# Another sequence of units in the first batch, with a newly written order of every engine

## The chip, the cores and the metric

The kernel runs on one core of a Trainium2 chip. Its engines are TensorE (PE in the profile; PEld are its weight loads), VectorE (DVE), ScalarE (ACT), GpSimd (POOL), and SyncE (SP), which here only issues transfers. The metric is the device time of one execution in microseconds (us). The kernel before ran three times: 225.64, 225.78 and 225.80 us, median 225.78 us.

## The reference, cut to what matters

```python
# q, k, v: (4 batches, 8 heads, 768 tokens, 64); centroids: (8, 16, 64)
q_assign = argmax(normalised(q) @ normalised(centroids))      # the same for k_assign
mask   = q_assign[:, :, :, None] == k_assign[:, :, None, :]
scores = where(mask, q @ k.T / 8, -1e9)
attn   = softmax(scores);  x = attn @ v                       # tokens x 512
h    = x @ w_in                                               # 512 -> 1024
solu = h * softmax(h)
ln   = (solu - mean) / sqrt(var + 1e-6) * g_ln
out  = ln @ w_out                                             # 1024 -> 512
```

All arrays are float32; the result is 3072 x 512.

## The kernel before, in words

Heads are worked in pairs: a batch has pairs 0 to 3. For each pair of heads, queries and keys are loaded, turned so that the head's 64 numbers lie on partitions, and written in bf16 into a tile `qk`. Sixteen (with a second group, 32) further rows of `qk` hold the one-hot cluster of each token, so that one matmul of 80 or 96 rows gives the score with its mask. The exponential of the score then goes through ScalarE, and a second matmul multiplies it with the values. The tokens' normalised result goes through the feed-forward part, one tile of 128 tokens at a time (24 tiles).

The code records every step as a named operation, and this document uses the names. A dotted name gives batch and pair, then the side (0 queries, 1 keys) and the head of the pair or the half.

| name | step | function, line | engine |
|---|---|---|---|
| `ld`, `lv` | load queries/keys, values | `load`, `load_apart` L374, `load_v` L527 | SP |
| `tp`, `xa` | batch 0: turn 128 x 384 on PE into the region `hreg`; copy it to `xt` | L386; `keep_tokens` L393 | PE; ACT or DVE |
| `xt` | later batches: turn on DVE | `turn` L407 | DVE |
| `ca` | cast `xt` into `qk` | `cast` L431, L433, L435 | POOL, DVE, ACT |
| `cl` | cluster scores | `clusters` L445, L450 | PE |
| `tb`, `mx`, `oh`, `ot` | turn back, maximum, one-hot, turn | L459, L472, L478/L484, L491/L494 | DVE |
| `pl`, `bl` | copy the one-hot rows into `qk`; blank 16 rows for the pair's second head | L506/L514; L523 | POOL, DVE, SP (a transfer); POOL, DVE |
| `cv` | cast values | L532 | POOL, DVE |
| `S n.k`, `E n.k` | bank k of unit n: scores, exponential | `scores` L601, `expo` L607 | PE; ACT |
| `V n.j`, `N g` | values of unit n; division for group g | L624; L636, L649 | PE; DVE |
| `su`, `sk`, `me`, `ce`, `wi` | preparation of the feed-forward weights | L574, L581, L584, L587, L552 | PE, DVE, POOL |
| `h`, `hm`, `ex`, `u` | x @ w_in, maximum, exponential, product | L710, L716, L722, L727 | PE, DVE, ACT, DVE |
| `bn`, `ag`, `at`, `al` | variance and factor | L738, L742, L748, L754/L757 | DVE, DVE, POOL, POOL |
| `tx`, `tu` | turn x, u by a transfer | `turn_x`, `f_turn` L732 | SP |
| `y`, `sc`, `ou` | u @ w_out, scaling, store | L771, L786/L788, L798 | PE, ACT or DVE, SP |

Units. A unit is one piece of scores: pair 0 of batch 0 has units 0 to 3 with six or three banks of 384 columns; all later units have three banks of 512 columns. In batch 0 the units of pairs 1 to 3 come as the list `FIRST` (L280) says: its entry (p, s) stands for two units, one for each head of pair p, with the s-th third of the queries. `BANKS` is the sequence of all score banks. `S` and `E` follow it strictly, and the `V` follow the units.

Rings. Scores have three PSUM banks (`ring_s`, L1012), so `S` of a bank waits for the `E` three banks earlier. The exponentials have nine tiles (`ring_e`), so `E` of a bank waits for the `V` that read the tile nine banks earlier. All values of a group share one PSUM tile `ops`, so the first `V` of a group waits for the `N` of the group before. The region `hreg` has three banks; in batch 0 each `tp` waits for the `xa` three before it.

Order. Nothing is scheduled at run time: each engine runs its instructions strictly in the order written in `ORDER`, one text for each engine, in which "S3 tp2" means the next three `S` and the next two `tp` (`queues`, L110). An operation whose input is late therefore holds up everything behind it on its engine. `AWAY` (L73 on) moves single operations from the engine that the code gives them by default to another that can run them. Feed-forward work (`h`, `y`) comes to PE only when the first batch is nearly through, from 46 us on.

Of the kernel before, what the change touches and what calls it, by code (L numbers as in the profile page):

```python
# [22 lines left out]
class Weave:  # L23
# [6 lines left out]
        ld4 lv si ld4 lv lg ld4 lv2 ld4 lo2 ld4 lo ld3 lo ld3 li4 tx ld3 lv3 tx ld4 tu ld9 lv ld tu  # L30
        tx ld3 tu ld3 ou ld2 ou ld tu ld12 tu ld4 lv ld2 ou tx ld3 tu ou ld2 tx lv ld tu ld4 tx ld
        tu ou2 ld lv ld4 tu ld4 tu ld ou ld7 pl ou ld lv2 ld3 tu lv tx ou tu lv pl ld4 ou2 tx lv tu
        tx ou tu pl2 tu2 tx tu tx ou2 tx ou tu tx2 ou tu2 ou2 tu2 ou6
# [8 lines left out]
    """
    ORDER["PE"] = """
        wm tp2 cp tp cl tp fl5 cl fl4 S3 tp2 S2 tp S cq S tp S2 tp2 S2 V3 S cl S tp2 V3 S gt S tp S
        tp S2 cl S2 V2 S V S2 tp S2 tp S2 V2 S V S2 cl S2 V2 S V2 S3 V S2 V2 S2 V S cl S3 su S2 V3 S
# [1 line left out]
        S h S V S V S h S2 V3 S2 V h S2 h V2 S y3 S2 h3 S3 y V3 h V S2 V2 S cl S3 h2 S2 V3 S y2 S V
        h2 S V y2 S h S V h S2 h S y3 S2 y V3 h S3 cl V2 S V S y S2 y2 S3 V3 S y S2 V3 S2 cl S V S2
        V2 S h S2 V2 S V S h S2 V2 cl V2 S3 y2 S V S2 V y S2 y V2 S3 h2 S V h S h S2 V h S V S V y2
        S h V y2 S2 V S h3 S cl V S2 V2 S h V cl S3 h2 V y V S3 y2 V S h V3 S y S h S2 h2 S3 V2 y h  # L50
        S V S2 y V3 y S3 h3 y S3 V3 S h S V S V cl S V S h S cl V2 S3 y V2 S y S2 y V2 S3 h y V S3 V
# [1198 lines left out]
```

## Time and profile before

| | us |
|---|---|
| median of three runs | 225.78 |
| the profiled execution | 225.95 |
| its span, first to last instruction | 223.9 |
| around the span (225.95 - 223.9) | 2.05 |
| PE busy in the span | 215.1 |
| DVE / ACT / POOL busy | 197.3 / 191.5 / 127.1 |

A busy PE isn't one at its peak: a score of 256 columns takes 264 ns in the mean there, but consecutive ones overlap. How far PE is from idle is better read from the distance of one matmul's start to the next. Rows of the timeline give start, duration, engine, line, operation, the tiles written and read with their shapes, a count, and in brackets the idle time of the engine before it with what ended it. One row can stand for several instructions that follow each other; its time is then that of the first start to the last end.

### The profile page before, as it was taken

The page shows a single profiled execution, that of the slowest core. Times are in us where ns is not written, and L with a number is a line of the kernel's source. Part 1 is how long each engine was busy: PE and PEld are TensorE (multiplying, and loading weights), DVE is VectorE, ACT ScalarE, POOL GpSimd, SP SyncE. Part 2 cuts the span into 40 slices and gives each one's busy share as a digit, 9 for nine tenths or more (in the row PEclk, how much of TensorE's full clock was granted, in tenths as well). Part 3 has the DMA queues.
Part 4 walks back from the last instruction along what each step waited for, and adds up shares of the span by engine and source line. Part 5 has one row for each costly group of instructions (what it writes and reads, how often), then busy time and mean ns, then how long its engine had stood idle before and what let it go on. Part 6 is the DMA issues. An engine that isn't in the chain of part 4 may idle for free.

```text
span 223.9 us, 6574 instructions
## 1 busy us (share of the span) xinstructions
PE 215.1 (96%) x2388; PEld 148.1 (66%) x2420; DVE 197.3 (88%) x359; ACT 191.5 (86%) x371; POOL 127.1 (57%) x247
## 2 busy tenths in 40 slices
PE   7899999999999999999999999999999999999993
PEld 3576756677667678776677667777677687754442
DVE  3799899899999989999998989887998889888981
ACT  3689999999998999998889899999999998982362
POOL 3489843964794999547668634943895413031331
PEclk9999999999999999999999999999999999999999
DMA  7998989999898989999999999199931433766622
GB/s 152 353 318 147 249 199 275 290 243 158 132 199 140 232 130 165 193 189 177 183 218 168 184 195 195 65 174 232 236 64 28 79 70 120 96 146 170 176 97 94
DMA packets 125679, 38.80 MB, mean 173 GB/s; under 512 B 115016, under 2 KB 121168, under 8 KB 125648
## 3 DMA queue, kind: packets, MB, share of 16 engines
q1 hardware_dynamic: 123904, 37.87, 80.6%
q10 hardware_dynamic: 1744, 0.52, 1.0%
q8 instruction: 19, 0.31, 0.6%
q14 instruction: 12, 0.10, 0.2%
HBM read 23.11 MB, written 6.29 MB: 131 GB/s over the span
## 4 chain that ended last, share of the span: by engine, by line
PE 86%; ACT 5%; DVE 3%; issue 3%; DMA 1%; POOL 1%; ACTq 0%; DVEq 0%; POOLq 0%
PE sps L601 28%; PE hreg L710 18%; PE yps L771 16%; PE ops L624 14%; ACT e L607 5%; PE csc L450 4%; PE hreg L386 2%; PE hreg L574 1%; PE hreg L771 1%; DMA c_all<-in_centroids_dram 1%; PE csc L445 1%; DVE bs L738 1%; DVE u L727 1%; ACT xt L393 0%; PE hreg L584 0%
## 5 line engine op out<-in xcount | busy, mean ns | idle before, releaser
L607 ACT ACTIVATE e<-sps 128x512 bf16<-128x512 f32 (+1 forms) x294 | 151.0, 599 | 12.2 <-PE sps L601 10.2
L601 PE MATMUL sps<-qk 80*128 80x256 bf16 (+5 forms) x636 | 93.8, 264 | 1.8 <-POOL qk L514 0.7
L601 PEld LDWEIGHTS <-qk 80*128 80x128 bf16 (+1 forms) x636 | 60.2, 121 | 27.9 <-issue 9.0
L624 PEld LDWEIGHTS <-e 128*128 128x128 bf16 x1152 | 50.4, 97 | 12.3 <-issue 1.9
L624 PE MATMUL ops<-v,e 128*128 128x65 bf16 x1152 | 55.0, 193 | 0.1
L710 PE MATMUL hreg<-w_in_sb,xT 128*128 128x512 bf16 x173 | 49.1, 379 | 1.1
L771 PE MATMUL yps<-w_out_c,uT 128*128 128x512 bf16 x171 | 46.4, 379 | 0.6
L727 DVE TENSOR_TENSOR u<-e_sb,hreg 128x1024 bf16<-128x1024 bf16 x24 | 29.0, 1210 | 4.9 <-ACT e_sb L722 4.7
L514 POOL COPY qk<-oht 32x384 f32<-32x384 f32 (+1 forms) x50 | 24.4, 488 | 15.8 <-DVE oht L494 13.6
L738 DVE BATCH_NORM_STATS2 bs<-u 128x6 f32<-128x512 bf16 x48 | 31.5, 676 | 0.2
L716 DVE TENSOR_REDUCE nmax<-hreg 128x1 f32<-128x1024 f32 x24 | 29.0, 1209 | 2.6 <-PE hreg L710 2.2
L722 ACT ACTIVATE e_sb<-hreg,nmax 128x1024 bf16<-128x1024 f32 x24 | 26.9, 1120 | 4.5 <-DVE nmax L716 4.4
L433 POOL CAST qk<-xt 64x768 bf16<-64x768 f32 (+1 forms) x31 | 26.1, 842 | 5.5 <-DVE xt L393 3.9
L771 PEld LDWEIGHTS <-uT 128*128 128x128 bf16 x200 | 18.2, 97 | 12.3 <-DVE uT L704 0.7
L754 POOL TENSOR_SCALAR esq<-es,mv 128x1 f32<-128x1 f32 x24 | 8.5, 355 | 29.0 <-DVE mv L742 20.8
L435 POOL TENSOR_SCALAR qk<-xt 64x768 bf16<-64x768 f32 (+1 forms) x28 | 23.0, 820 | 1.7
L710 PEld LDWEIGHTS <-xT 128*128 128x128 bf16 x192 | 16.8, 97 | 9.4 <-issue 0.6
L407 DVE STREAM_TRANSPOSE xt<-raw 128x768 f32<-128x768 f32 x24 | 22.6, 953 | 0.2 <-DMA raw<-in_q_dram 0.2
L748 POOL TENSOR_SCALAR es<-esum 128x1 f32<-128x1 f32 x24 | 5.3, 221 | 27.6 <-ACT e_sb L722 27.1
L649 DVE TENSOR_TENSOR x<-ops,den 128x256 bf16<-128x256 f32 (+1 forms) x39 | 18.9, 486 | 1.3
L757 POOL TENSOR_TENSOR alpha<-esq,halves 128x1 f32<-128x1 f32 x24 | 13.5, 561 | 2.0
L786 ACT ACTIVATE y<-yps,alpha 128x512 f32<-128x512 f32 x13 | 9.0, 692 | 6.4 <-PE yps L771 6.0
(80 smaller groups left out, 170.1 us busy)
## 6 DMA issues: line engine op xcount, KB each, us to landing
vf<-in_v_dram SPq DMA_DIRECT2D x16, 384.0 KB, 4.4
out_dram<-y SPq DMA_DIRECT2D x23, 256.0 KB, 2.7
raw<-in_q_dram SPq DMA_DIRECT2D x50, 96.0 KB, 3.7
raw<-in_k_dram SPq DMA_DIRECT2D x50, 96.0 KB, 3.0
w_g<-in_moe_w_out_dram SPq DMA_DIRECT2D x4, 512.0 KB, 5.3
w_st<-in_moe_w_in_dram SPq DMA_DIRECT2D x4, 512.0 KB, 5.9
raw<-in_q_dram SPq DMA_DIRECT2D x3, 384.0 KB, 6.3
raw<-in_k_dram SPq DMA_DIRECT2D x3, 384.0 KB, 6.8
```

Source lines behind the costliest of these rows:

```text
L433: VEC[e].tensor_copy(dst, src)
L435: VEC[e].tensor_scalar(dst, src, scalar1=inv_C, scalar2=1.0, op0=Alu.mult, op1=Alu.mult)
L514: ins = VEC[e].tensor_copy(dst.bitcast(F32), src.bitcast(F32).unsqueeze(1) .to_broadcast([NB, 2, n // 2]))
L601: nc.tensor.matmul(sps_[n, k][:, c0:c0 + w], side(b, h // 2, 1, h % 2, keys)[r], side(b, h // 2, 0, h % 2, slice(s0 * P, s0 * P + w))[r])
L607: nc.scalar.activation(es[n, k][:, :w], sps_[n, k][:, :w], Act.Exp, scale=exp_scale, bias=-exp_scale)
L624: nc.tensor.matmul(opss[g][:, s, :VW], es[n, k][:, c0:c0 + P], v1[slot(b, h // 2)][:, h % 2, kt, :VW], start=(kt == 0), stop=(kt == n_t - 1))
L710: uses(nc.tensor.matmul(hreg[:, at(f, f2)[1], :], xTs[f][:, dc, :], w_in_sb[:, dc, f2 * FF2:(f2 + 1) * FF2], start=(dc == 0), stop=(dc == ...
L716: uses(nc.vector.tensor_reduce(ff[f, "nmax"][:], pair_of(f), axis=AXY, op=Alu.max, negate=True), *both(f))
L722: uses(nc.scalar.activation(ff[f, "e"][:], pair_of(f), Act.Exp, bias=ff[f, "nmax"][:], accum_out=ff[f, "esum"][:]), *both(f))
L727: uses(nc.vector.tensor_tensor(ff[f, "u"][:], ff[f, "e"][:], pair_of(f), op=Alu.mult), *both(f))
L738: nc.vector.bn_stats(ff[f, "bs"][:, f2, :], ff[f, "u"][:, f2, :])
L771: ins = nc.tensor.matmul(dst, ff[f, "uT"][:, at(f, f2)[0] * (n_fc // 2) + c, :], w_out_c[:, fc, cols], start=(fc == 0), stop=(fc == n_fc - 1))
```

## The change

The list `FIRST` changes, and with it every text of `ORDER` and both the members and the engines of `AWAY`. No operation is added or removed; no size, tile or buffer changes.

```diff
-    FIRST = [(p, s) for p in range(1, n_pair) for s in range(2)] + [(p, 2) for p in range(1, n_pair)]
+
+    FIRST = [(1, 0), (1, 1), (2, 0), (3, 0), (2, 1), (3, 1), (1, 2), (2, 2), (3, 2)]
```

Written out, the list before is (1,0), (1,1), (2,0), (2,1), (3,0), (3,1), (1,2), (2,2), (3,2). The two lists differ in one exchange: the first third of pair 3 and the second third of pair 2 change places. Pair 3 is then needed from unit 10 on, where it was needed from unit 12 on; units 10 to 13 are renumbered, and units 4 to 9 and from 14 on are what they were.

The core of the order's diff, with the beginning of each text:

```diff
     ORDER["POOL"] = """
-        po z ca2 pl2 cv z bl pl2 ca z ca pl2 ca z2 ca3 cv ca cv ca pl3 sg ca cv2 pl3 ca2 gs pl ca cv
-        ca wi ca pl2 wi3 bl ca pl2 cv at cv pl ca pl al bl at cv ca pl ca pl cv ca3 al at ca al ca
...
+        po ca2 pl2 ca bl zo pl2 bl ca pl ca4 cv2 ca pl2 z ca2 gs ca pl3 z ca pl3 cv2 pl sg z2 ca3 pl
+        wi4 pl2 ca3 pl2 at pl2 cv bl2 cv at z cv ca al ca al at al pl2 cv pl2 ca4 at cv pl ca pl3 al
...
     ORDER["PE"] = """
-        wm tp2 cp tp cl tp fl5 cl fl4 S3 tp2 S2 tp S cq S tp S2 tp2 S2 V3 S cl S tp2 V3 S gt S tp S
...
+        wm tp2 cp tp cl tp fl5 cl fl4 S3 cq tp S2 tp S2 tp S tp S2 tp2 V3 S2 cl S2 V3 S gt tp S tp
...
     ORDER["DVE"] = """
-        cn cb xa ca tb mx oh ot pl2 tb mx oh ot xa3 bl cf cv xa zo xa2 tb ca mx oh gk N ot tb pl mx
...
+        cn xa cb ca tb mx oh ot pl2 tb mx oh ot cv pl xa cv xa3 ca cf tb mx N oh xa cv ot gk pl xa
...
     ORDER["ACT"] = """
-        wa xa2 ca2 xa ca2 E12 xa2 E6 xa E58 ex E12 ex E8 ex E8 ex E3 sc E5 ca E2 ex E25 ex E9 sc E6
...
+        wa xa2 ca xa ca3 E9 xa2 E9 xa2 E5 xa E3 xa E50 ex E10 ex E7 ex E2 sc E3 ca E ex ca E6 sc E8
...
```

With the names filled in, this is where the orders differ at the places that the next part speaks of (a semicolon parts before and after):

- PE up to the first values: `S1.2 cq S0.3 tp0.1.1.1 S0.4 S0.5 tp0.2.0.0 tp0.2.0.1 S1.3 S1.4 V0.0`; now `S1.2 S0.3 tp0.1.1.0 S0.4 tp0.1.1.1 S0.5 S1.3 tp0.2.0.0 tp0.2.0.1 V0.0`.
- PE before unit 25: `S24.0 S24.1 V22.0 V22.1 V23.0 S24.2 S25.0`; now `S24.0 S24.1 h2.0.0 h2.0.1 S24.2 S25.0`, with the three values behind `S25.1`.
- ACT at the start: `xa0.0.0.0 xa0.0.1.0 ca0.0.0.0.0 ca0.0.0.1.1 xa0.0.1.1 ...`; now `xa0.0.1.0 xa0.0.0.1 ca0.0.1.0.0 xa0.0.1.1 ...`. Before `E6.0` ACT had three more copies (`xa0.2.1.0`, `xa0.2.1.1` before `E2.0`, `xa0.3.0.0` before `E3.0`); now it has six: `xa0.2.0.0`, `xa0.2.0.1` between `E0.5` and `E1.3`, `xa0.2.1.1`, `xa0.3.0.0` before `E3.0`, `xa0.3.1.0` before `E3.5`, `xa0.3.1.1` before `E4.2`.
- DVE at the start: `cb xa0.0.0.1 ca0.0.1.0.0 tb0.0.0`; now `xa0.0.0.0 cb ca0.0.0.0.0 tb0.0.0`. Behind `ot0.0.1`: `xa0.1.0.0 xa0.1.0.1 xa0.1.1.0`; now `cv0.0.0 pl0.0.1.1.0 xa0.1.0.0 cv0.0.1 xa0.1.0.1 xa0.1.1.0`.
- DVE around pair 3: `N2 xt1.0.0 mx0.3 xt1.0.1 N3 oh0.3 ot0.3`; now `tb0.3 mx0.3 oh0.3 ot0.3 N2 pl0.3.1.0 ca0.3.1.1 xt1.0.0 xt1.0.1 N3`. The cast `ca0.3.1.1` was POOL's.
- DVE around the first product: `u0 oh1.1 ot1.1`; now `oh1.1 N9 u0 ot1.1`.
- POOL behind the weight casts: `wi3 bl1.0 ca1.0.1.1 pl1.0.0.0 pl1.0.0.1 cv1.0.0`; now, behind `wi3`, `pl1.0.1.1 pl1.0.0.0 ca1.1.0.0 ca1.1.0.1 ca1.1.1.0 pl1.0.0.1 pl1.1.1.0 at0 pl1.1.1.1 pl1.1.0.1 cv1.0.0 bl1.0`.
- SP: the values of pairs 1 and 2 in batch 0 are loaded ahead of the keys of pair 3; `pl1.1.0.0` stands behind `tu0`.
- The end of PE's order, from `ptx23`, has one `h` less in it, which now stands before; behind that the two are the same.

Between engines, 63 operations change place:

| from | to | operations |
|---|---|---|
| POOL | DVE | 18: 8 `cv`, 5 `ca`, 3 `pl`, 2 `bl` |
| DVE | POOL | 13: 4 `pl`, 4 `bl`, 2 `ca`, 2 `cv`, `zo` |
| DVE | ACT | 10: 5 `xa`, 2 `ca`, 3 `sc` |
| ACT | DVE | 6: 2 `xa`, 1 `ca`, 3 `sc` |
| POOL | SP | 8 `pl` (`pl1.1.0.0` and seven of batches 2 and 3) |
| SP | POOL | 2 `pl` |
| POOL | ACT | 4 `ca` (1.2.0.0, 1.2.0.1, 3.0.1.0 and one of pair 0) |
| ACT | POOL | 2 `ca` |

In all DVE has 10 `xa` before and 7 now, 5 `cv` before and 11 now, 4 `ca` before and 6 now; ACT has 6 `xa` before and 9 now, 5 `ca` before and 8 now; POOL has 212 operations before and 199 now; SP has 4 `pl` before and 10 now. PE has the same 732.

More of the change, by code (lines that the diff above doesn't have):

```diff
@@ L29 @@
     ORDER["SP"] = """
[L30 to L33, printed above, removed]
+        ld4 lv si ld4 lg ld lv2 ld lv ld3 lo ld3 lo ld lo ld5 lo ld4 li4 tx ld5 lv ld tx ld7 tu lv
+        ld2 pl tx ld tu ld3 ou ld2 tu ld lv2 ld2 tu ld ou lv ld13 tu ld2 lv ld3 ou tx ld3 tu ld2 ou
@@ L47 @@
[L47 to L51, printed above, removed]
```

70 lines of the change are left out of this document (39 added, 31 removed).

## Prediction

> **What bounds the kernel now.** I read the page's header, its busy times and the chain of waits first.
>
> ```profile
> span 223.9 us, 6574 instructions
> PE 215.1 (96%) x2388; PEld 148.1 (66%) x2420; DVE 197.3 (88%) x359; ACT 191.5 (86%) x371; POOL 127.1 (57%) x247
> PE 86%; ACT 5%; DVE 3%; issue 3%; DMA 1%; POOL 1%; ACTq 0%; DVEq 0%; POOLq 0%
> ```
>
> The chain that ends last runs through PE for 86% of the span. The change gives PE the same 732 operations, so time can only come from stretches in which PE waits. Where these are, the stage windows say (columns: busy us of PE, PEld, DVE, ACT and POOL, counts in brackets, PE's granted clock, DMA share, GB/s).
>
> ```profile
> 10.00:55.00 45.00, 43.70 (x544) 30.32 (x547) 41.22 (x85) 42.01 (x89) 30.59 (x54) 1.00 1.01 241
> 55.00:210.00 155.00, 153.40 (x1740) 108.49 (x1768) 142.50 (x242) 139.06 (x265) 90.01 (x170) 1.00 0.82 156
> ```
>
> From 55 to 210 us PE is busy for 153.40 of 155 us: a new order can hardly gain there, it can only lose. The first 55 us are different. ACT is busy for 42.01 of 45 us there, and until feed-forward work comes PE has little to do that doesn't follow from an exponential. ACT's timeline shows where it waits.
>
> ```profile
> 10.52 3.56 ACT L607 ACTIVATE e<-sps 128x384 bf16<-128x384 f32 x9 [1.11 <-PE sps L601]
> 14.80 1.25 ACT L607 ACTIVATE e<-sps 128x384 bf16<-128x384 f32 x3 [0.72 <-PE ops L624]
> 16.44 0.86 ACT L393 COPY xt<-hreg 128x384 f32<-128x384 f32 x2 [0.39 <-PE hreg L386]
> ...
> 25.91 5.50 ACT L607 ACTIVATE e<-sps 128x512 bf16<-128x512 f32 x11 [0.16 <-PE sps L601]
> 31.57 1.57 ACT L607 ACTIVATE e<-sps 128x512 bf16<-128x512 f32 x3 [0.16 <-PE sps L601]
> 33.33 4.69 ACT L607 ACTIVATE e<-sps 128x512 bf16<-128x512 f32 x9 [0.18 <-PE sps L601]
> 38.39 6.23 ACT L607 ACTIVATE e<-sps 128x512 bf16<-128x512 f32 x12 [0.38 <-PE sps L601]
> 44.79 5.55 ACT L607 ACTIVATE e<-sps 128x512 bf16<-128x512 f32 x11 [0.16 <-PE sps L601]
> ```
>
> Between the first exponential and 55 us ACT waits 0.72 + 0.39 + 0.16 + 0.16 + 0.18 + 0.38 + 0.16 = 2.15 us in all. So two things decide: when `E0.0` starts, and what ACT has to do beside exponentials until PE is full of feed-forward work.
>
> **The change, part by part.** Sums are made against the profiled execution, 225.95 us (span 223.9 and 2.05 around it); the median of the runs is 0.17 lower, and a difference found here is laid on the median, 225.78.
>
> *Start of the first score.* These rows are the way to it.
>
> ```profile
> 6.74 0.53 PE L450 MATMUL csc<-xt,c_bd 128*32 128x192 f32 x8
> 6.85 0.56 DVE L393 COPY xt<-hreg 128x384 f32<-128x384 f32 x1 [0.66 <-PE hreg L386]
> 7.32 0.34 DVE L435 TENSOR_SCALAR qk<-xt 64x384 bf16<-64x384 f32 x1
> 7.59 0.37 DVE L459 STREAM_TRANSPOSE cst<-csc 128x192 f32<-128x192 f32 x1
> 10.16 0.65 PE L601 MATMUL sps<-qk 80*128 80x384 bf16 x3 [0.73 <-POOL qk L514]
> ```
>
> The cluster scores end at 7.27, but their turning stands behind a copy and a cast on DVE and starts at 7.59. Both go to ACT; what DVE gets in their place (`xa0.0.0.0`, `ca0.0.0.0.0`) reads the first turning, which ACT copies today ahead of all this. The turning then starts at about 7.31, and all steps behind it on the way keep their lengths: -0.28 at `S0.0` and `E0.0`. Bounds: 0, if PE's clusters start later, and -0.28.
>
> *The first values.* Behind that, DVE gets work ahead of the copies that free `hreg`.
>
> ```profile
> 9.25 0.58 DVE L514 COPY qk<-oht 32x192 f32<-32x192 f32 x2
> 11.35 1.45 DVE L393 COPY xt<-hreg 128x384 f32<-128x384 f32 x3
> 13.49 0.51 DVE L532 CAST v<-vf 128x384 bf16<-128x384 f32 x1
> 13.14 0.82 PE L386 MATMUL hreg<-ident_f,raw 128*128 128x128 f32 x6
> 14.12 0.73 PE L624 MATMUL ops<-v,e 128*128 128x65 bf16 x18
> ```
>
> Two value casts of 0.51 and one placing of 0.58 / 2 = 0.29, 1.31 us, come in front of the third copy. It ends at 12.80 - 0.28 + 1.31 = 13.83. `tp0.2.0.1` needs the bank that it frees, and takes 0.82 less the 0.33 by which the other `tp` starts sooner, 0.49. `V0.0` stands right behind it: 13.83 + 0.49 = 14.32, against 14.12. The gain of 0.28 is gone there and 0.20 is lost. Every `E` behind the ninth tile waits for these values. Bounds: -0.28 (the copies in time after all) and +0.20.
>
> *Three more copies on ACT.* By shape, a copy takes
>
> ```profile
> L393 ACT COPY xt<-hreg 128x384 f32<-128x384 f32 x6 | 2.8, 477 | 1.3 <-PE hreg L386 1.3
> ```
>
> 3 x 0.477 = 1.43 us on the engine that paces this stretch. Two of the six now stand in the wait of 0.72 before `E1.3`, and the wait of 0.39 before the old copies has no copy to wait for any more: 1.43 - 1.11 = +0.32. With the +0.20, `E6.0` (25.91 before) comes 0.52 later. Behind it ACT waits 0.16 + 0.16 + 0.18 + 0.38 + 0.16 = 1.04 us more, each time since PE had a block of other work (`cl`, `su`, `me`) in front of a score. An ACT that runs half a microsecond later gives PE that much lead over it, and these waits shrink; I take 0.40 of them, between 0 (PE falls behind equally) and 1.04. Left at 55 us: +0.12.
>
> *Pair 3 one unit sooner.* `S10.0` is now pair 3 and needs `ca0.3.1.1`.
>
> ```profile
> 32.96 0.83 POOL L435 TENSOR_SCALAR qk<-xt 64x768 bf16<-64x768 f32 x1
> 31.08 0.83 PE L601 MATMUL sps<-qk 80*128 80x256 bf16 x6
> 31.26 0.98 DVE L491 STREAM_TRANSPOSE w_out_c<-w_out_c 128x768 bf16<-128x768 bf16 x1
> 27.91 0.98 DVE L407 STREAM_TRANSPOSE xt<-raw 128x768 f32<-128x768 f32 x1 [0.21 <-DMA raw<-in_q_dram]
> 27.05 0.18 DVE L636 RECIPROCAL den<-ops 128x4 f32<-128x4 f32 x1 [0.38 <-PE ops L624]
> 27.27 0.42 DVE L649 TENSOR_TENSOR x<-ops,den 128x256 bf16<-128x256 f32 x1
> ```
>
> That cast ended on POOL at 33.79, and `S10.0` is the second bank of the PE row, at 31.31. `ot0.3` ended at 32.24. Two turnings of 0.98 and two divisions of 0.60 now come behind it: 32.24 - 3.16 = 29.08. Then come one division (0.60), a placing and the cast, for which I set POOL's times, 0.50 (a row below) and 0.83: 31.01. It is ready 0.3 us before `S10.0`, so the exchange costs nothing, and gains nothing either: the same scores, banks and values pass in another sequence. Without that cover it costs what the second rival says.
>
> *A wait at unit 25.* `bl1.0` now stands behind the placings of pair 1, which wait for `ot1.1`.
>
> ```profile
> 51.60 1.22 DVE L727 TENSOR_TENSOR u<-e_sb,hreg 128x1024 bf16<-128x1024 bf16 x1 [0.34 <-ACT e_sb L722]
> 53.33 0.58 DVE L494 STREAM_TRANSPOSE oht<-oh 128x384 bf16<-128x384 bf16 x1
> 54.04 0.50 POOL L514 COPY qk<-oht 32x384 f32<-32x384 f32 x1 [1.70 <-DVE oht L494]
> 51.65 0.24 POOL L748 TENSOR_SCALAR es<-esum 128x1 f32<-128x1 f32 x1 [2.93 <-ACT e_sb L722]
> 57.11 0.41 POOL L523 MEMSET qk<- 16x384 f32 x1
> 55.84 0.62 PE L601 MATMUL sps<-qk 80*128 80x256 bf16 x4
> ```
>
> `ot1.1` right behind `u0` ends at 51.60 + 1.22 + 0.58 = 53.40, and POOL can start 0.13 behind it, as today (54.04 after 53.91): 53.53. Three placings of 0.50, the small operation (0.24), a value cast (0.51, as on DVE above) and the blanking (0.41) make 2.66: `bl1.0` ends at 56.19, or somewhat later with the steps between them. `S25.0` is the second bank of the PE row, at 55.84 + 0.22 = 56.06. The wait is 0.13 if its place on PE stays, and less as two parts of `h` take the place of three values in front of it; I take +0.10. Bounds: 0, and 0.64, if `ot1.1` keeps its old end at 53.91. Behind a blocked `S25.0` stand the bank `S25.1` and the values of units 22 and 23, which need nothing more from POOL but wait in PE's order.
>
> *The rest.* From 55 to 210 us I take 0. ACT gets four casts and three scalings more and gives one cast and three scalings away, out of 155 - 139.06 = 15.9 us that it is idle there. Bounds: -1.6, all that PE is idle there (155 - 153.40), and +0.6, one more wait like that at unit 25. Eight placings go to SP and two leave it; there one lands late:
>
> ```profile
> qk<-oht SPq DMA_DIRECT2D x4, 48.0 KB, 2.2
> ```
>
> 2.2 us against 0.50 on POOL, which is 1.7 later but off POOL's queue; all but `pl1.1.0.0` are in batches 2 and 3, where a pair is prepared units ahead. The end of PE's order is the same but for one `h`: 0.
>
> Sum: 0.20 + 0.32 - 0.40 + 0.10 = +0.22, 226.00 us. With one term at a time at its bound (the waits behind `E6.0` at 1.04 or 0, unit 25 at 0.64) it is 225.4 to 226.6; the low bound of the rest belongs to the faster rival.
>
> A POOL cast can be stretched by DVE: a 64 x 768 cast took 1.15 us at 34.31 while DVE cast the same shape from 34.03 to 34.77.
>
> ```profile
> 34.31 1.15 POOL L433 CAST qk<-xt 64x768 bf16<-64x768 f32 x1
> 34.03 0.74 DVE L433 CAST qk<-xt 64x768 bf16<-64x768 f32 x1
> ```
>
> [...]
>
> **The rivals.** *Faster: ACT's waits fill up.* If the copies go into waits entirely, all 2.15 us of them are gone for 1.43 us of copies, and the first score comes 0.28 sooner: 1.43 - 2.15 - 0.28 = -1.00, 224.78. For it: DVE is relieved of copies and its 41.22 of 45 us loosen. Against it: the waits behind 25 us come from PE's blocks, which the change only puts elsewhere.
>
> *Slower: the exchange takes away pair 3's cover.* If `ca0.3.1.1` is no sooner than today (33.8), `S10.0` waits 33.8 - 31.3 = 2.5 us; three banks at 0.49 (5.50 / 11) keep ACT going for 1.5 of it: +1.0, 226.8. It decides once the cast ends after 31.3, with 0.3 us to spare. That the pair is needed sooner but isn't ready sooner is also the case in which the change doesn't do what it says.
>
> *Slower: ACT is the bound and takes the copies in full.* 1.43 - 0.28 = +1.15, 226.93. It decides once the copies on ACT wait for their `tp`, so that they fill no wait. For it: ACT is the busiest engine but PE from 10 to 55 us. Against it: two copies stand exactly in the widest wait. [...]
>
> **How the numbers follow.** About 0.2% (0.45 us) can be told from no change here. Forecast 226.00: 0.40, of it 0.26 within that, 0.10 slower, 0.04 faster. ACT's waits filled: 0.30, faster. Pair 3 late: 0.10, slower. Copies in full: 0.20, slower. So faster 0.34, same 0.26, slower 0.40. The forecast's own range is 225.4 to 226.6; the range for 8 in 10 goes from 224.7, where the faster rival lies, to 227.3, the fullest copies with the wait at unit 25.
>
> **What would show it.** In the changed profile: `S0.0` near 9.88 and `V0.0` near 14.3; ACT's row before the fourth set of 384-column exponentials with copies where 0.72 us of waiting was; the first 512-column exponential near 26.4; a wait of PE for POOL's blanking near 56.2; 155 us of full PE behind it. A first 512-column exponential before 25.5 would make the forecast wrong to the fast side, a PE wait over 0.5 us for a cast near 31 or anywhere behind 60 us to the slow side.

## The result, and the profile after

| | before | after |
|---|---|---|
| median of five runs, us | 225.78 | 228.96 |
| lowest and highest run, us | 225.64 to 226.15 | 228.68 to 229.74 |
| the profiled execution: span, us | 223.9 | 227.6 |

After / before is 1.0149, with a 95% interval of 1.0124 to 1.0174: 2.8 to 3.9 us slower, where 226.0 was predicted. (Times are medians of all runs; ratios, here and below, compare the means and leave out a run that is over 1.5% above the fastest of its kernel.) The page's header, the busy times and the chain of waits of the kernel after:

```profile
span 227.6 us, 6619 instructions
PE 219.9 (97%) x2420; PEld 149.0 (65%) x2420; DVE 198.8 (87%) x360; ACT 194.0 (85%) x377; POOL 119.4 (52%) x234
PE 84%; ACT 5%; DVE 5%; issue 3%; DMA 1%; SPq 0%; ACTq 0%; DVEq 0%
```

and its windows (columns as before):

```profile
10.00:55.00 45.00, 43.76 (x548) 29.94 (x541) 40.47 (x79) 41.91 (x90) 30.79 (x51) 1.00 1.02 233
55.00:210.00 155.00, 154.66 (x1763) 108.15 (x1761) 142.24 (x244) 141.06 (x270) 81.37 (x158) 1.00 0.81 156
```

The windows hardly tell the two apart, and two things in them mislead. Before, PE has 2388 matmuls on the page, after 2420, though its operations are the same 732: 32 records are missing before, all of `h` and `y` (`e1` below, with the same orders as before, has 2420 again). Work whose record is missing looks like idle time, so PE had less room from 55 to 210 us than 153.40 of 155 says, if any. And a busy PE is not an advancing one (in `e1` below it is busy for 3.50 of 3.50 us at a granted clock of 0.50). What shows the loss is PE's lag: I add up, in PE's written order, a usual length for each operation (a bank of scores 0.22, values 0.19, a part of `h` or `y` 0.43, clusters 0.79, and so on), and compare the starts of the two kernels at equal sums, as a mean over 1.6 us of work. Positive is later than the profiled execution before, at equal work done (times across the top are those of the kernel before):

| PE's lag, us | 11 | 25 | 27 | 55 | 61 | 135 | 175 | 195 | 215 |
|---|---|---|---|---|---|---|---|---|---|
| after | 0.76 | 1.10 | 1.64 | 1.64 | 2.21 | 2.43 | 2.82 | 3.11 | 3.20 |
| `e2`: new orders, old list | -0.45 | 0.05 | 0.59 | 0.59 | 1.16 | 1.38 | 1.79 | 2.08 | 2.17 |
| `e1`: old orders, new list | 0.57 | 0.56 | 0.56 | 5.85 | 5.85 | 5.84 | 5.84 | 5.84 | 5.85 |
| `g1`: new orders to 47 us, then old | -0.54 | -0.04 | 0.52 | 0.46 | 0.46 | 0.46 | 0.46 | 0.46 | 0.46 |
| `k2`: new orders to 62 us, then old | -0.48 | 0.02 | 0.56 | 0.56 | 1.13 | 1.13 | 1.13 | 1.13 | 1.14 |
| `g2`: old orders to 47 us, then new | 0.53 | 0.52 | 0.52 | 0.56 | 1.13 | 1.28 | 1.60 | 1.93 | 1.98 |
| `k1`: old, two copies on ACT | 0.18 | 0.67 | 0.67 | 0.67 | 0.67 | 0.67 | 0.67 | 0.67 | 0.67 |

The other rows belong to experiments told below. Lateness comes in at five places: up to the first scores, between 11 and 27 us, at 57 to 60 us, in small steps behind that, and behind the last product. Where the old order follows in this table (`e1`, `g1`, `k1`, `k2`), the lag is then level to a hundredth: what is lost once is not made good. (In `h3` below, which is 3 us late, it even grows by another 0.33 behind 100 us.)

*The first scores.* PE's timeline of the kernel after:

```profile
6.00 0.85 PE L388 MATMUL hreg<-ident_f,raw 128*128 128x128 f32 x3
6.78 0.87 PE L452 MATMUL csc<-xt,c_bd 128*32 128x192 f32 x8
7.58 0.90 PE L388 MATMUL hreg<-ident_f,raw 128*128 128x128 f32 x3
8.27 1.27 PE L818 MATMUL idle_p<-w_out_c 128*128 128x256 bf16 x5
9.47 0.87 PE L452 MATMUL csc<-xt,c_bd 128*32 128x192 f32 x8
10.28 0.75 PE L818 MATMUL idle_p<-w_out_c 128*128 128x256 bf16 x4
10.87 0.65 PE L603 MATMUL sps<-qk 80*128 80x384 bf16 x3
```

The cluster scores take 0.87 us where they took 0.53 before, the idle matmuls are twice as far apart (0.21 us from 8.27 us on; before 0.11 from 7.59 on), and `S0.0` stands behind them until 10.87. The same orders in another execution (`e2`):

```profile
5.93 0.52 PE L388 MATMUL hreg<-ident_f,raw 128*128 128x128 f32 x3
6.38 0.54 PE L452 MATMUL csc<-xt,c_bd 128*32 128x192 f32 x8
...
7.87 0.61 PE L452 MATMUL csc<-xt,c_bd 128*32 128x192 f32 x8
...
9.66 0.65 PE L603 MATMUL sps<-qk 80*128 80x384 bf16 x3 [0.64 <-POOL qk L516]
```

PE comes to its full pace early or late in both kernels: of seven profiles with the old first 10 us three show the cluster scores at 0.53 us, of eleven with the new first 10 us eight at 0.53 to 0.60. It is worth 0.6 to 1.2 us at `S0.0` (10.87 and 9.66 us here), and by my estimate, which no run shows by itself, it spreads the runs of both kernels (before: 225.35 to 226.9 for most runs over all chips used). So from here on the new order's first part is read in `e2` and the old one's in a profile with the same early pace.

*Up to 55 us.* ACT's timeline in `e2`:

```profile
13.60 0.94 ACT L395 COPY xt<-hreg 128x384 f32<-128x384 f32 x2
14.54 1.25 ACT L609 ACTIVATE e<-sps 128x384 bf16<-128x384 f32 x3
16.41 1.45 ACT L609 ACTIVATE e<-sps 128x384 bf16<-128x384 f32 x3 [0.62 <-PE sps L603]
18.10 1.37 ACT L609 ACTIVATE e<-sps 128x384 bf16<-128x384 f32 x3 [0.25 <-PE sps L603]
19.35 0.87 ACT L395 COPY xt<-hreg 128x384 f32<-128x384 f32 x2
...
21.94 0.58 ACT L395 COPY xt<-hreg 128x384 f32<-128x384 f32 x1
...
23.80 0.50 ACT L395 COPY xt<-hreg 128x384 f32<-128x384 f32 x1
24.16 1.62 ACT L609 ACTIVATE e<-sps 128x512 bf16<-128x512 f32 x3
25.94 4.03 ACT L609 ACTIVATE e<-sps 128x512 bf16<-128x512 f32 x8 [0.16 <-ACT e L609]
30.43 3.04 ACT L609 ACTIVATE e<-sps 128x512 bf16<-128x512 f32 x6 [0.47 <-PE sps L603]
33.75 5.15 ACT L609 ACTIVATE e<-sps 128x512 bf16<-128x512 f32 x10 [0.27 <-PE sps L603]
39.13 2.56 ACT L609 ACTIVATE e<-sps 128x512 bf16<-128x512 f32 x5 [0.23 <-PE sps L603]
41.86 9.14 ACT L609 ACTIVATE e<-sps 128x512 bf16<-128x512 f32 x18 [0.17 <-PE sps L603]
```

ACT's waits behind the first exponential sum to 0.62 + 0.25 + 0.16 + 0.47 + 0.27 + 0.23 + 0.17 = 2.17 us; before they were 2.15. In sum the copies came on top and took no wait away. Up to `E6.0` (25.91 before, 26.43 in `e2`) the waits shrank only from 1.27 to 1.03 us, since the old one of 0.72 is gone but one of 0.62 stands in front of `E2.0`; behind it they grew from 0.88 to 1.14.

*At 57 to 60 us*, the kernel after, POOL, ACT and PE:

```profile
57.64 0.77 POOL L525 MEMSET qk<- 16x384 f32 x2
57.82 0.93 PE L603 MATMUL sps<-qk 80*128 80x256 bf16 x6
57.94 1.21 ACT L724 ACTIVATE e_sb<-hreg,nmax 128x1024 bf16<-128x1024 f32 x1
...
58.59 0.92 PE L626 MATMUL ops<-v,e 128*128 128x65 bf16 x24
...
59.03 2.65 ACT L609 ACTIVATE e<-sps 128x512 bf16<-128x512 f32 x5
...
59.78 0.38 PE L603 MATMUL sps<-qk 96*128 96x256 bf16 x2 [0.27 <-ACT e L609]
```

`bl1.0` is the first of the two blankings. PE passes it almost without a wait. PE then waits for something else: `S25.2` needs the bank of `E24.2`, and `E24.2` now stands on ACT behind `ex1` (57.94) and starts at 59.03. Before, `ex1` stood two exponentials later, and the same score, the last bank of this row, came without a wait:

```profile
56.92 0.60 PE L601 MATMUL sps<-qk 96*128 96x256 bf16 x4
```

*The end.* The last products on PE and the last scaling on DVE, after:

```profile
221.95 1.92 PE L773 MATMUL hreg<-w_out_c,uT 128*128 128x256 bf16 x16 [0.16 <-DVE uT L706]
...
224.34 0.48 DVE L790 TENSOR_SCALAR e_sb<-hreg,alpha 128x256 f32<-128x256 f32 x1 [2.33 <-PE hreg L773]
```

2.39 us from the first row's start to the second's. Before it was 2.03:

```profile
218.76 1.92 PE L771 MATMUL hreg<-w_out_c,uT 128*128 128x256 bf16 x16 [0.16 <-DVE uT L704]
...
220.79 0.48 DVE L788 TENSOR_SCALAR e_sb<-hreg,alpha 128x256 f32<-128x256 f32 x1 [1.97 <-PE hreg L771]
```

### The profile page after: what moved, and what is told of

It reads as the page before. It is cut to its first block, busy times and chain, and to the rows that moved or that the text cites. A ratio compares the mean times of both kernels' runs of the same rounds, so it can differ in the third digit from the quotient of the medians.

```text
span 227.6 us, 6619 instructions
## 1 busy us (share of the span) xinstructions
PE 219.9 (97%) x2420; PEld 149.0 (65%) x2420; DVE 198.8 (87%) x360; ACT 194.0 (85%) x377; POOL 119.4 (52%) x234
## 4 chain that ended last, share of the span: by engine, by line
PE 84%; ACT 5%; DVE 5%; issue 3%; DMA 1%; SPq 0%; ACTq 0%; DVEq 0%
PE sps L603 26%; PE hreg L712 17%; PE yps L773 16%; PE ops L626 14%; PE csc L452 5%; ACT e L609 4%; PE hreg L388 2%; DMA raw<-in_k_dram 1%; DVE u L729 1%; PE hreg L576 1%; PE hreg L773 1%; ACT e_sb L724 1%; PE csc L447 1%; DVE xt L395 1%; DVE bs L740 1%
## 5 line engine op out<-in xcount | busy, mean ns | idle before, releaser
L603 PE MATMUL sps<-qk 80*128 80x256 bf16 (+5 forms) x636 | 95.5, 264 | 1.2 <-ACT e L609 0.7
L626 PE MATMUL ops<-v,e 128*128 128x65 bf16 x1152 | 54.4, 193 | 0.0
L712 PE MATMUL hreg<-w_in_sb,xT 128*128 128x512 bf16 x192 | 52.7, 379 | 0.0
L773 PE MATMUL yps<-w_out_c,uT 128*128 128x512 bf16 x184 | 49.1, 379 | 0.1
L516 POOL COPY qk<-oht 32x384 f32<-32x384 f32 (+1 forms) x43 | 21.0, 488 | 24.5 <-DVE oht L496 18.2
L435 POOL CAST qk<-xt 64x768 bf16<-64x768 f32 (+1 forms) x27 | 21.2, 784 | 6.1 <-ACT xt L395 3.7
L437 POOL TENSOR_SCALAR qk<-xt 64x768 bf16<-64x768 f32 x27 | 23.1, 857 | 2.2 <-ACT xt L395 0.6
L461 DVE STREAM_TRANSPOSE cst<-csc 128x384 f32<-128x384 f32 (+1 forms) x17 | 9.3, 550 | 4.2 <-PE csc L452 3.0
```

The lines of the kernel that those rows point to most:

```text
L435: VEC[e].tensor_copy(dst, src)
L437: VEC[e].tensor_scalar(dst, src, scalar1=inv_C, scalar2=1.0, op0=Alu.mult, op1=Alu.mult)
L603: nc.tensor.matmul(sps_[n, k][:, c0:c0 + w], side(b, h // 2, 1, h % 2, keys)[r], side(b, h // 2, 0, h % 2, slice(s0 * P, s0 * P + w))[r])
L626: nc.tensor.matmul(opss[g][:, s, :VW], es[n, k][:, c0:c0 + P], v1[slot(b, h // 2)][:, h % 2, kt, :VW], start=(kt == 0), stop=(kt == n_t - 1))
L712: uses(nc.tensor.matmul(hreg[:, at(f, f2)[1], :], xTs[f][:, dc, :], w_in_sb[:, dc, f2 * FF2:(f2 + 1) * FF2], start=(dc == 0), stop=(dc == ...
L773: ins = nc.tensor.matmul(dst, ff[f, "uT"][:, at(f, f2)[0] * (n_fc // 2) + c, :], w_out_c[:, fc, cols], start=(fc == 0), stop=(fc == n_fc - 1))
```

## The experiments

**One list, one order at a time; the idle PE; three repairs.** All four ran on one chip, beside 11 runs of the kernel before (median 225.72).

`e1`, the kernel before with the new list:

```diff
-    FIRST = [(p, s) for p in range(1, n_pair) for s in range(2)] + [(p, 2) for p in range(1, n_pair)]
+    FIRST = [(1, 0), (1, 1), (2, 0), (3, 0), (2, 1), (3, 1), (1, 2), (2, 2), (3, 2)]
...
     ORDER["DVE"]:  -  pl2 ca N pl xt mx N sk
                    +  pl2 ca pl N xt mx N sk
```

> The kernel before with the new list of units, and one placing (pl0.3.0.1) moved one place forward on DVE so that the units can run at all. Theory 1 (the newly written order loses the time, the exchange of units does not): pair 3's last cast stays at about 33.8 us on POOL where S10.0 would want it at 31.3, PE waits some 2.5 us for it, and 1.0 us of that is left at the end: 226.8, and no more than 227. Rival (the exchange itself loses it): at least 228.5.

Measured 230.67 us (228.23 to 231.78), ratio 1.0174 (1.0130 to 1.0218). Both sides of the expectation were wrong in size, and the rival's threshold was reached; but what is seen is the mechanism that theory 1 named, at another price. PE's timeline:

```profile
31.64 0.39 PE L601 MATMUL sps<-qk 80*128 80x256 bf16 x2
34.71 1.01 PE L601 MATMUL sps<-qk 80*128 80x256 bf16 x4 [2.67 <-DVE qk L506]
35.65 1.94 PE L574 MATMUL hreg<-w_g,w_out_c 128*32 128x512 f32 x8
```

and the windows around it (the third column from the right is PE's granted clock):

```profile
32.50:35.00 2.50, 0.29 (x2) 0.26 (x3) 2.41 (x5) 0.23 (x1) 1.91 (x4) 0.81 0.91 202
35.00:38.50 3.50, 3.50 (x19) 1.11 (x18) 1.22 (x2) 1.36 (x3) 1.02 (x1) 0.50 1.05 240
38.50:42.00 3.50, 3.50 (x54) 3.08 (x52) 1.63 (x4) 2.69 (x6) 1.83 (x2) 0.66 0.98 379
```

PE waits 2.67 us for pair 3 (expected 2.5), and then runs at half clock: `su0` takes 1.94 us where it takes 1.06 (a row of the kernel after has 1.06, too). The lag grows by 5.85 - 0.56 = 5.3 us, not by 1.0. That is the price in this execution. Two of the six runs, 228.23 and 228.71 us, have a mean granted clock of 1.00: they are 2.5 and 3.0 us over 225.72, about the wait itself. The other four, this one among them, have 0.983 to 0.990 and take 230.6 to 231.8 us.

`e2`, the changed kernel with the old list: the first two lines of the diff above, turned round.

> The changed kernel with the old list of units, all written orders as in the changed kernel. Theory 1 (the written order loses the time): 228.7 to 229.2, as the changed kernel. Rival (the exchange itself): near 226.

Measured 228.86 us, ratio 1.0131 (1.0111 to 1.0151), as the changed kernel. So in the new order the exchange of units is worth nothing either way; the written order makes the loss. In the profiles, too, the kernel after lies behind `e2` by a constant 1.03 to 1.05 us from 25 us to the end, which is the later full pace at its start. The new order also carries what the exchange needs: without it, `e1` shows, the exchange costs 2.5 us or more.

`e3`, the changed kernel with three idle matmuls in PE's first wait:

```diff
-        wm tp2 cp tp cl tp fl5 cl fl4
+        wm tp fl3 tp cp tp cl tp fl5 cl fl4
```

> The changed kernel with three idle matmuls of 256 columns between the first two turnings on PE, where PE waited 0.56 us for the keys. Theory 2 (PE waits so long there that it goes on at half pace until 10.6 us, in part of the executions): full pace from about 6.8 us on, S0.0 at 9.9 to 10.2 instead of 10.87, all runs at or under the lower of the two levels that the changed kernel showed, 228.7 or up to 0.5 lower. Rival (the half pace has nothing to do with this wait): S0.0 at 10.8 in the profile or runs at both levels, 228.7 and 229.7, again.

Measured 228.80 us (228.61 to 229.57), ratio 1.0136 (1.0113 to 1.0159). In the profile PE is at full pace from 6.0 us and `S0.0` starts at 9.75, but `e2` without the idle matmuls shows the same (9.66), so the profile can't tell; and two of the six runs of `e3` are over 229, where `e2` has one. Theory 2 found no support (the last part of this document says what the clock records add).

`e4`, three single moves in the changed kernel:

```diff
     DVE  -  xa cv xa3 ca cf tb              +  xa cv xa3 cf ca tb
     PE   -  S2 su S2 V S V S V2 S2 cl S3    +  S4 V S V S V2 S2 cl S2 su S
     ACT  -  E50 ex E10 ex E7 ex             +  E50 ex E12 ex E5 ex
```

> The changed kernel with three operations put elsewhere: cf on DVE one cast sooner (so that cl0.1 does not wait), su0 on PE behind S10.2 instead of S8.0 (so that E8.1 does not wait), ex1 on ACT behind E25.0 instead of E24.1 (so that S25.2 does not wait). Theory 3 (lateness at these places is never made good): 0.5, 0.5 and 0.5 us less, 227.3 to 227.8. Rival (each wait is only found again at the next place, since PE or ACT is full there): at most 0.4 us less, 228.5 or more.

Measured 232.10 us, ratio 1.0270 (1.0241 to 1.0299): 3 us worse. `cf` brought 0.2 us at 15 us, which was gone by 19. `su0` behind `S10.2` put the wait there, larger (lag 1.54 at 31 us; `e2` 0.41). With `ex1` later, `u1` came later, and `h2.1.0`, which needs it, stands early in the new PE order:

```profile
59.95 0.40 PE L603 MATMUL sps<-qk 96*128 96x256 bf16 x2
62.09 1.59 PE L712 MATMUL hreg<-w_in_sb,xT 128*128 128x512 bf16 x4 [1.75 <-DVE u L729]
```

The granted clock was 0.56 from 62 to 65.5 us in this profile, and the lag rose from 1.72 to 5.38. The place of `ex1` is thus bound from both sides in the new order.

**Where it is lost: grafts of the two orders.** Here every engine's order consists of the operations that one kernel starts before a set time, in that kernel's order and on its engines, and of all the others as in the other kernel; the list is the old one, which `e2` allows. On one chip, beside 30 runs of the kernel before (median 226.23, most of them near 225.6 or near 226.5). ACT's text for the four, from the kernel before:

```diff
-        wa xa2 ca2 xa ca2 E12 xa2 E6 xa E58 ex E12 ex E8 ex E8 ex E3 sc E5 ca E2 ex E25
+g1      wa xa2 ca xa ca3 E9 xa2 E9 xa2 E5 xa E3 xa E50 ex E12 ex E8 ex E8 ex E3 sc E5 ca E2 ex E25
+g2      wa xa2 ca2 xa ca2 E12 xa2 E6 xa E58 ex E10 ex E7 ex E2 sc E3 ca E ex ca E6 sc E8 ex E25
+g3      wa xa2 ca xa ca3 E12 xa2 E6 xa E58 ex E12 ex E8 ex E8 ex E3 sc E5 ca E2 ex E25
+g4      (on ACT as g1)
```

`g1`, new to 47 us:

> The old list of units; every operation that started before 47 us (401 of them) in the changed kernel's order and on its engine, all later ones in the order and on the engine of the kernel before. Theory A (two separate losses, one before 47 us, a larger one behind it that belongs to the later part of the order): the front's lag of 0.55 us, measured on PE at equal work, is all that is left: 226.0 to 226.5. Rival B (the late part is slow because it starts late): 228 or more.

Measured 226.58 us, ratio 1.0021 (0.9993 to 1.0050); lag 0.46, level to the end. Theory A by the lag; the time is 0.08 over its range, and its interval takes in no change at all.

`g2`, old to 47 us:

> The other way round: up to 47 us as in the kernel before, then the changed kernel's order and engines. Theory A: 0.6 at 57 to 60 us, 1.0 from there to 215, 0.6 behind the last product, so 225.7 + 2.2 = 227.9, give or take 0.4. Rival B: at most 226.2.

Measured 228.75 us, ratio 1.0106 (1.0061 to 1.0150). Its profile has the late pace (lag 0.52 from the first scores on); from there 0.6 at 57 to 60 us and 0.85 up to the last products (lag 1.98: their row starts at 220.74, before at 218.76). Theory A again by the lag; the time is 0.45 over its range, but 2.5 over the kernel before on this chip, where 2.2 was expected. Behind the last product nothing is lost, against the theory's 0.6: 0.38 us from the last matmul's start to the last scaling, as before; 0.73 after.

`g3`, new to 10.3 us:

> The kernel before with only the first 10.3 us (67 operations) in the changed kernel's order and engines. Theory (the head gains 0.3 to 0.45 us at S0.0, and PE passes it on to the end): 225.3 to 225.5. Rival (the copies and casts behind it use it up by 25 us): 225.6 to 225.8.

Measured 225.66 us, ratio 0.9979 (0.9952 to 1.0006). Undecided: the gain expected is no larger than what the pace of the first 10 us makes from run to run. It is also the best of all versions run, and not shown to be faster than the kernel before.

`g4`, new to 25 us:

> As the first of this set, but only up to 25 us (211 operations) in the changed kernel's order. PE stood at +0.05 us there in the run with the old list of units. Theory A: 225.5 to 225.9. Rival (the 0.5 us that ACT lost by 26 us come from copies that stand before 25 us): 226.2 or more.

Measured 226.86 us, ratio 1.0039 (1.0012 to 1.0066); lag 0.09 at 25 us and 0.54 from 29 us on, with `E6.0` at 26.46. The rival: what makes `E6.0` late stands before 25 us. `su0`, which is back at its old place here, makes no difference to what is left.

**Four single causes.** On one chip, beside 11 runs of the kernel before (median 226.19, highest 228.12).

`h1`, the changed kernel with three more instructions on DVE:

```diff
     nc.vector.memset(halves[:, 1:2], -0.5)
+    spare = const.tile([P, 1], F32, name="spare")
+    for _ in range(3):
+        nc.vector.memset(spare[:], 0.0)
```

> The changed kernel with three more tiny instructions at the start of DVE (a memset of one number per partition each), nothing else. In the changed kernel DVE's last scaling starts 0.40 us after the semaphore of the last product has come, in the kernel before 0.05 us; the run with the old front and the new rest, whose DVE has three recorded instructions more, shows 0.05 as well. Theory (the 0.35 us hangs on where the instruction lies in DVE's stream, not on the order): 0.05 again and the end 0.35 us sooner, 228.2 to 228.6. Rival (something in the order holds it up): 0.40 as before, 228.6 to 229.

The times are too unquiet to tell (229.70 us, 228.21 to 231.48, ratio 1.0142, 1.0087 to 1.0197; in the profile PE waits 1.6 us for a transfer at 143 us). The place itself is clear:

```profile
224.18 1.92 PE L773 MATMUL hreg<-w_out_c,uT 128*128 128x256 bf16 x16 [0.16 <-DVE uT L706]
...
226.21 0.48 DVE L790 TENSOR_SCALAR e_sb<-hreg,alpha 128x256 f32<-128x256 f32 x1 [1.97 <-PE hreg L773]
```

2.03 us, as before the change, where the changed kernel had 2.39. In all five profiles with the changed kernel's number of instructions on DVE (452 recorded, semaphores counted) the scaling comes 0.73 to 0.75 us behind the start of the last matmul, in the other thirteen, with 444 to 455 of them, 0.38.

`h2`, three operations moved by one place:

```diff
     ACT  -  E50 ex E10 ex E7 ex             +  E50 ex E11 ex E6 ex
     ACT  -  E11 ex E7 ex E9 ex E7 ex E7 ex  +  E11 ex E7 ex E9 ex E8 ex E6 ex
     DVE  -  u cv bl N hm cv bn              +  u cv bl hm N cv bn
```

> The changed kernel with one operation moved by one place at each of three spots where PE waits for a score's exponential that stands behind a feed-forward exponential: ex1 on ACT behind E24.2, hm15 on DVE in front of N31, ex17 on ACT behind E87.1. Theory (these three waits are the steps in PE's lag): its lag against the kernel before grows less at 57 to 60 us (by 0.3 to 0.6), at 173 to 176 (by 0.25) and at 186 to 189 (by 0.15): together 0.6 to 0.9 us off, 227.9 to 228.3. Rival (PE finds each wait again within a few units, since ACT is full): 228.6 or more.

Measured 231.06 us, ratio 1.0211 (1.0161 to 1.0261): each move made its place worse. PE's timeline at the three:

```profile
59.36 0.38 PE L602 MATMUL sps<-qk 96*128 96x256 bf16 x2 [0.41 <-ACT e L608]
60.13 1.04 PE L711 MATMUL hreg<-w_in_sb,xT 128*128 128x512 bf16 x4 [0.39 <-DVE u L728]
...
175.17 0.54 PE L625 MATMUL ops<-v,e 128*128 128x65 bf16 x12 [0.71 <-DVE x L650]
...
189.84 1.04 PE L711 MATMUL hreg<-w_in_sb,xT 128*128 128x512 bf16 x4 [0.39 <-DVE u L728]
```

The wait for an exponential became one for the product `u` behind it, or for the division that had been put back. Neither theory nor rival as for the places (the time is in the rival's range): the waits are not found again elsewhere, they grow where they are (lag +1.2 instead of +0.6 at 57 to 60 us).

`h3`, the graft `g4` with `xa0.3.1.0` and `xa0.3.1.1` on DVE, behind `xa0.3.0.1` and `oh0.2`:

```diff
     ACT  -  xa2 E5 xa E3 xa E50             +  xa2 E58
     DVE  -  pl xa pl cv tb mx oh N          +  pl xa2 pl cv tb mx oh xa N
```

> The kernel before with the changed kernel's first 25 us, as in the run before, but with the last two copies of pair 3's keys (xa0.3.1.0, xa0.3.1.1) on DVE, where the kernel before has them. Theory (these 0.95 us of copies on ACT are what makes the sixth unit's exponential 0.5 us later): E6.0 at or before 26.0 and the lag of 0.5 us gone, so 0.3 to 0.5 us under the kernel before. Rival (DVE is as full there: pair 2's and pair 3's one-hot rows come later and PE waits for them): lag 0.5 or more.

Measured 228.80 us, ratio 1.0100 (1.0052 to 1.0149). The rival, more than that: `cl0.3` on PE waits for the second copy in the middle, with the scores of unit 5 behind it, and the lag is 1.93 at 25 us and 2.99 at 37.

`h4`, the kernel before with the new list and pair 3's cast in time:

```diff
     DVE  -  tb0.3 pl0.2.1.1 N2 xt1.0.0 mx0.3 xt1.0.1 N3 oh0.3 ot0.3 ...
          +  tb0.3 pl0.2.1.1 mx0.3 oh0.3 ot0.3 N2 pl0.3.1.0 ca0.3.1.1 pl0.3.0.0 xt1.0.0 xt1.0.1 N3 ...
     POOL -  pl0.3.1.1 ca0.3.1.1 cv0.3.1     +  pl0.3.1.1 cv0.3.1
```

> The kernel before with the new list of units, and on DVE pair 3's one-hot rows ahead of a division and two turnings, with its last cast (ca0.3.1.1) behind them instead of on POOL; nothing else moved. The cast should then end before 31.5 us. Theory (the exchange itself costs nothing once the cast is in time): 225.5 to 226.1. Rival (the sequence of units itself loses time): 226.7 or more.

Measured 228.84 us, ratio 1.0134 (1.0074 to 1.0194). The cast was in time (30.50), but no clean test came of it: PE's first wait is for the division `N2`, which now stands behind the one-hot rows, and the next for the turning behind that. Two of the six runs take 231.2 us with a mean granted clock of 0.978, the other four 228.2 to 228.9 with 0.992 to 1.00.

```profile
29.17 0.36 PE L624 MATMUL ops<-v,e 128*128 128x65 bf16 x6 [1.69 <-DVE x L649]
...
32.14 1.70 PE L450 MATMUL csc<-xt,c_bd 128*32 128x384 f32 x8 [0.78 <-DVE xt L407]
```

What `h4` gives otherwise is the old order with an early full pace: its lag is -0.43 and level up to 25 us.

**What was still open: the copies alone, and the parts behind 60 us.** On one chip, beside 26 runs of the kernel before (median 225.82).

`k1`, the kernel before with two copies given to ACT:

```diff
     ACT  -  xa2 E6 xa E58 ex                +  xa2 E6 xa E5 xa E3 xa E50 ex
     DVE  -  pl mx xa2 oh xa cv N            +  pl mx xa oh cv N
```

> The kernel before with only the two last copies of pair 3's keys (xa0.3.1.0, xa0.3.1.1) taken from DVE to ACT, at the places that the changed kernel gives them (in front of E3.5 and of E4.2). Theory (ACT is the bound between 17 and 26 us and takes copies in full): 2 x 0.477 = 0.95 us more at E6.0, and PE's lag stays so to the end: 226.4 to 226.8. Rival (the copies go into waits of ACT, as the prediction's sum had it for the greater part): at most 0.2 us, 225.6 to 225.9.

Measured 226.63 us, ratio 1.0031 (1.0005 to 1.0057). The time lies in the theory's range. The lag lies between theory and rival: it goes from 0.18 to 0.67 at 25 us and stays, 0.49 us for 0.95 us of copies, about half of what the whole first part loses.

`k2`, new to 62 us (ACT: `... xa E50 ex E10 ex E10 ex E8 ex ...`, then as before):

> The changed kernel's order and engines for all that started before 62 us, the kernel before's behind it, with the old list of units. Theory (the loss at 57 to 60 us belongs to the order of these few microseconds, and is kept): PE's lag as with the seam at 47 us plus 0.6, then level to the end; 226.8 to 227.3. Rival (it is made good behind it when the old order follows): as with the seam at 47 us, 226.2 to 226.6.

Measured 227.44 us, ratio 1.0063 (1.0038 to 1.0089). Lag 0.56 at 55 us and 1.13 from 59 us to the end. The theory by the lag; the time is 0.14 over its range.

`k3`, old to 62 us (ACT: `... E58 ex E12 ex E6 ex E sc E3 ...`, then as after):

> The kernel before up to 62 us, the changed kernel's order and engines behind it. Theory (the order behind 62 us loses about 1.0 us by itself, in small steps at 70, 125, 174 and 186 to 195 us, though nothing is late at its start): 226.6 to 227.0, with the same steps in PE's lag. Rival (these steps are only the follow-on of the lateness at 60 us): 225.6 to 225.9, no steps.

Measured 228.30 us, ratio 1.0105 (1.0068 to 1.0142). The seam itself loses 1.6 us at 62 to 65 us (`S28.1` behind `h3.0.1`), so its time tells nothing. Steps at 174 (1.68 to 1.94) and 186 to 195 us (to 2.27) are there as in `e2`, but behind a lateness of 1.7. The clean comparison is `k2` with `g2`: both stand at 1.13 at 61 us; with the old order behind it the lag stays at 1.13, with the new one it goes to 1.93 at 195 us and 1.98 at the last products. So the steps belong to the order behind 62 us, and not to the lateness before it.

`k4`, the same with three casts on POOL:

```diff
     ACT  -  ca1.2.0.0 ca1.2.0.1 ca3.0.1.0
     POOL +  ca1.2.0.0 ca1.2.0.1 (ahead of ca1.2.1.0), ca3.0.1.0 (ahead of ca3.0.1.1)
```

> As the run before, with the three casts of later pairs that the changed kernel gives to ACT behind 62 us where POOL had them (ca1.2.0.0, ca1.2.0.1, ca3.0.1.0) back on POOL. Theory (these casts make the steps at 70 and 125 us): these two steps of 0.1 each are gone, those at 174 and 186 to 195 stay. Rival (the steps have nothing to do with the casts): all stay, or new ones come since POOL is later.

Measured 228.88 us, ratio 1.0115 (1.0071 to 1.0159). From 66 to 75 us the lag grows by 0.28 instead of 0.47, but between 95 and 105 us by 0.23 where it had been level. The rival: POOL pays it back later.

One of the steps can be read in `e2`. ACT waits for a maximum and then keeps PE's banks for 1.2 us:

```profile
174.27 1.11 ACT L724 ACTIVATE e_sb<-hreg,nmax 128x1024 bf16<-128x1024 f32 x1 [0.29 <-DVE nmax L718]
```

`hm15` stands on DVE behind a cast, a blanking and the division `N31`. `S83.0` starts at 176.11 and `S83.1` at 176.50, each 0.05 to 0.15 behind the end of the exponential that frees its bank (`E82.0` 175.96, `E82.1` 176.45), and the lag grows by 0.27.

## Why the prediction was wrong, point by point

Its sum was +0.22. In its own terms, with the times of the first part counted from the start of `cl0.0.0`, so that the pace of PE before it drops out (old order: the kernel before and `k3`, which agree to 0.02; new: `e2` and `k2`):

| term | predicted | measured | from |
|---|---|---|---|
| `S0.0` | -0.28 | -0.14 | 3.42 before, 3.28 after |
| `V0.0` | +0.20 | +0.11 | 7.38, 7.49 |
| `E6.0` | +0.52 | +0.88 | 19.17, 20.05 |
| ACT's waits behind `E6.0` | -0.40 | about 0 | lag 0.94 at 55 us (0.59 in `e2`, -0.35 in `k3`) |
| pair 3 one unit sooner | 0 | 0 | `e2` as the changed kernel |
| unit 25 | +0.10 | +0.57 | `k2`, 55 to 61 us |
| the rest to 215 us | 0 | +0.85 to +1.0 | `g2` and `e2`, 61 us to the last products |
| behind the last product | 0 | +0.36 | 2.03, 2.39 |

0.94 + 0.57 + 1.0 + 0.36 = 2.9, against 3.1 of `e2` over its runs of before (228.86 - 225.72).

- *The start.* The turning of the cluster scores starts 0.25 us sooner behind them, as said (0.31 before, 0.06 now). But the way from there to `ot0.0.0` takes 1.35 instead of 1.24, since its one-hot product takes 0.52 instead of 0.42; the placing on POOL that `S0.0` waits for starts 0.93 behind `ot0.0.0` both times. So 0.14 was left. "All steps behind it keep their lengths" was wrong.
- *ACT's copies.* This is the first of the two steps that failed by more than their bounds. I counted 1.11 us of waits that the copies could fill. The two copies before `E1.3` did fill theirs, but a wait of 0.62 came in front of `E2.0`, and the two at 22 and 24 us met no wait. The rival "ACT is the bound and takes the copies in full" (+1.15) described it: +0.94 at 55 us, and `k1` shows half of it with two copies alone. Behind 60 us `g1` and `k2` keep every hundredth of their lag. (A level lag alone doesn't tell PE from ACT or DVE, at 141 and 142 of 155 us after, as the engine without room.) The prediction also calls `E6.0` the first exponential of 512 columns, and counts the wait in front of it among those behind it. `E4.0` is the first: a row of the timeline prints the shape of its first instruction. The sum doesn't hang on that.
- *"These waits shrink"* failed with it. An ACT that runs late was to give PE a lead; but PE waits for ACT's exponentials in turn, through three banks, and both came late together. The waits stayed at 2.17 us in sum.
- *Pair 3.* In the kernel after, the cast ended at 31.62, 1.6 us before `S10.0` started (33.20). The step held. The second rival, the lost cover, had the right wait (2.67 in `e1`; 2.5 predicted) and the wrong price: 5.3 us in that profile, 2.5 to 3.0 in the two runs at full clock, instead of 1.0. Three banks did not cover 1.5 us of it.
- *Unit 25.* I named the meeting of `bl1.0` and `S25.0`, and it was where I put it, later by PE's lag (blanking at 57.64, score at 58.11), at next to no cost. In the same stretch `ex1` stands two exponentials sooner, and by the rows above that is what costs 0.57, six times as much as I took. No run took this loss away: `e4` and `h2` moved `ex1` and lost more. I had priced this stretch for POOL's queue and not for ACT's.
- *The rest, 0.* This is the largest failure: up to 1.4 us with the end. I took 153.40 of 155 us as little room to gain and let the loss be one more wait of 0.6 at most. But a full PE is just where every small wait adds up: four steps of 0.1 to 0.4 us did. Nor does the order of PE decide it alone; the two steps read here, at 58 and 174 us, come by their rows from where ACT and DVE put `ex` and `hm` between other work, though moving these by one place (`h2`) only made other waits. The cause of the steps at 70, 125 and 186 to 195 us stays open. The 0.36 behind the last product belongs to where the last scaling stands in DVE's stream, and not to the order of the work (`h1`).

## What to carry to other kernels

Where one engine is full for 70% of the span, a new written order can't be priced by its beginning: a lateness that it makes on that engine, anywhere, can be kept to the end (0.46 to 1.13 us here, to the hundredth), so the long full stretch is where to look for losses. Compare two orders by the lag of the full engine at equal work, not by busy times, and find the place by joining the first part of one to the second part of the other. In an order this tight don't expect to mend it by single moves: `e4`, `h2` and `h3` each moved what was late and lost 1 to 3 us more.

## What the runs showed of the hardware that I had not expected

- *PE's pace at the start.* In programs with the same first 10 us PE comes to full pace early or late; before that three turnings take 0.85 to 0.90 us (the kernel after, up to 8.5 us) instead of 0.52 (`e2`, at 5.93 us). The windows show a granted clock of 1.00 throughout (0 to 10 us of the kernels before and after), but the clock record in the traces only begins with the full clock, at 4.04 to 6.76 us in eleven profiles and at 9.15 to 10.60 us in seven, and the views count the time without a record as 1.00. In the kernel before the record begins at 6.66 us, just ahead of the cluster scores that take 0.53 us (6.74); in the kernel after at 10.60, where the starts of the idle matmuls come 0.11 us apart (10.65) instead of 0.21 (8.27). What makes it early or late is not shown. Filling a wait of PE with idle matmuls (`e3`) showed no effect, but its record begins where that of `e2` does (5.75 and 5.78 us), so it is no test.
- *Half clock behind a wait.* After a wait of 2.67 us (`e1`) PE's granted clock was 0.81, 0.50 and 0.66 in the windows above, that is 0.19 x 2.5 + 0.50 x 3.5 + 0.34 x 3.5 = 3.4 us less than at full clock, as much as 6.8 us at half clock would take away. After 1.75 us (`e4`) it was 0.56 for 3.5 us. After waits of 1.69 (`h4`) and 1.6 us (`h1`) the clock shown stayed at 1.00, though two other runs of `h4` have 0.978. So half clock does not stand behind each wait of this size; what decides it is not shown, and four cases are too few for a threshold.
- *The place of an instruction.* DVE's last scaling starts 0.05 us (the kernel before) or 0.40 us (the kernel after) after its semaphore, by whether three instructions more stand in DVE's stream (`h1`; `g2` has three more recorded ones too). What the engine does in these 0.35 us is not shown.
